# A two-layer H3 (FFT convolution) and MLP kernel: the shift filter goes to TensorE and GpSimd, with a new load order, new homes for the spectra, an inverse transform by halves and finer first blocks

## The chip, the cores and the metric

The kernel runs on one core of one Trainium2 chip. A core has five engines with an instruction queue each: TensorE (PE in the profile; its weight loads are shown apart as PEld), VectorE (DVE), ScalarE (ACT), GpSimd (POOL) and SyncE (SP), which here issues every DMA. The metric is the device time of one execution in microseconds (us). All data are bf16 in on-chip memory; matmul results stand in PSUM as fp32, and only ScalarE and VectorE take them out ("evict").

## The reference

Input is one sequence of 2048 positions and 512 channels. Two layers of an H3 mixer and an MLP follow each other, with the same weights both times:

```python
def _A_ref(q, k, v, shift_k, ssm_k, ssm_D):          # ks = 4, L = 2 * S
    for t in range(ks):                              # causal filter of 4 taps, per channel
        k_shift = k_shift + k_pad[:, t:t + S, :] * shift_k[:, ks - 1 - t][None, None, :]
    kv = k_shift * v
    y = irfft(rfft(kv_pad) * rfft(kf_pad))[:S]       # long causal convolution with ssm_k
    y = y + kv * ssm_D
    return q * y
def _B_ref(x, w1, b1, w2, b2):                       # D = 512, F = 1376
    return gelu(layernorm(x) @ w1 + b1) @ w2 + b2
x = A_q
x = x + _A_ref(layernorm(x), A_k, A_v, ...);  x = x + _B_ref(layernorm(x), ...)
x = x + _A_ref(layernorm(x), A_k, A_v, ...);  x = x + _B_ref(layernorm(x), ...)
```

k, v and the filters are the same in both layers, so y (without q) is computed once and used twice.

## The kernel before, in words

**The front: the convolution.** Channels are taken in four chunks of 128, positions as 16 slices of 128 (position = 16 p + a for partition p, slice a). The long convolution is a transform of length 4096 written as matmuls in two stages forward and two stages back.

1. *The filter's spectrum H.* ssm_k is loaded, ssm_D is added to its first tap on GpSimd (L550), TensorE transposes it (L565), `stage1` multiplies by cosine and sine tables (L580, 16 tiles of 16 matmuls), `stage2` by the table S2 (4 MB, eight loads at L495, matmuls at L593, 16 tiles). Each tile's result is evicted by ScalarE or VectorE (`evac`, L503 and L504). H is then copied by four DMAs with the two halves of its partitions exchanged into HS (real and imaginary part change places).
2. *The shift filter, kv.* Chunks 0 and 1 (`PE_CH`) go through TensorE: k comes transposed by a DMA transpose (L537), GpSimd builds diagonal matrices of the taps (L557), and `shift_pe` adds up four diagonal matmuls a slice in PSUM (L620); VectorE multiplies by v while evicting (L627). Chunks 2 and 3 go through VectorE (`shift_dve`): four multiplications, three additions over 128x2048 and two multiplications by v over 128x1024 a chunk, all at L498, the line of the helper `tt`.
3. *kv's spectrum and the product.* `s1x` runs `stage1` on each chunk into R_GX, `products(hf)` runs `stage2` on two chunks at a time (16 tiles in all, 8 a half), evicts each tile to one of three buffers (R_XB) and multiplies it on VectorE into H and into HS (L498, two products of 128x1024 a tile).
4. *The inverse.* `inverse1(hf)` (L681, 16 tiles of 16 matmuls) writes Z, whose rows hold the columns of both halves side by side, over the place of R_GX; the second inverse stage (L728, eight tiles of four matmuls with 512 columns) writes y.

**The MLP.** Each layer goes through four blocks of four slices. A block does the statistics of x (L746, L748 on VectorE; L752 and L754 on GpSimd for the inverse root), normalises (L760), multiplies by y and adds to x (L498), does the statistics again, normalises into a buffer, transposes it (on TensorE, L798 and an eviction at L806, for the very first block; by a DMA transpose, L790, for all others), then 44 matmuls with W1 (L817), GELU on ScalarE (L822), 44 matmuls with W2 (L835) and the add to x on VectorE (L839). In layer 2 each block's result is written out by one DMA.

**What sets the order.** The program lists its operations with what they read and write; `Prog.schedule` then plays them through with the written durations (`dur`) and gives each engine a fixed order, by earliest start and then by the longest chain behind. DMAs come in program order among those that are ready. Operations that name two engines (`BOTH`) go to the one that ends sooner. PSUM has eight banks; a `Tile` takes two (front) or one (MLP), from a `Pool` with a cap. `sync` and `emit` turn it into five instruction streams with semaphore waits. On the chip each engine, SP too, keeps its order; a late operand holds up everything behind it on that engine. Each GpSimd instruction also waits for the end of the one before it.

**Where things lie.** One array of 105856 bf16 elements a partition is divided by hand, and places are used again: S2's place holds the MLP's activations later; v's place holds x (loaded from q); k's places hold W1 and the inverse table T2; the shift filter's scratch (R_TMP) holds W2; the filter's stage-1 output R_G shares a place with HS, kv's stage-1 output R_GX shares one with Z, kv itself (R_KV) with y (R_YT). A load into a place waits until its last reader is done.

Of the kernel before, what the change touches and what calls it, by code (L numbers as in the profile page):

```python
# [22 lines left out]
class Pool:  # L23


    def __init__(self, nb, cap):
        self.nb, self.cap, self.used = nb, cap, 0
# [17 lines left out]
class Prog:  # L45
# [5 lines left out]
    LAT = 130.0  # L51

    def __init__(self, nc):
        self.nc = nc
        self.ops = []
        self.state = {}
        self.nodes = [(-1, None)]
        self.cache = {}

# [60 lines left out]
    def op(self, eng, fn, dur, reads=(), writes=(), tile=None, dma=None, prio=0.0, nbytes=0, after=()):  # L120
        o = Op()
# [3 lines left out]
        o.extra = prio  # L125
# [47 lines left out]

    def schedule(self):
# [29 lines left out]
        while done < n:  # L204
            best = None
            for e in free:
                te = max(free[e], 0.0)
                cand = None
                for o in ready[e]:
# [3 lines left out]
                    new = [x for x in o.tile if x.base is None]  # L213
                    if new:
# [4 lines left out]
                    k = (s, -o.prio, o.i)  # L219
                    if cand is None or k < cand[0]:  # L220
                        cand = (k, o)
# [4 lines left out]
                if best is None or (cand[0][0], cand[0][0] + d) < best[0]:  # L226
                    best = ((cand[0][0], cand[0][0] + d), e, o, cand[0][0])
# [191 lines left out]
PE_CH = (0, 1)  # L419


def bass_interleave_layers__ssm_conv_h3__mixer_channel_mlp__prompt_kernel(
# [85 lines left out]
    E1 = {ACT: 950.0, DVE: 1200.0}  # L508
# [23 lines left out]
    for i, c in enumerate(PE_CH):  # L532
# [4 lines left out]
        P.op(SP, lambda e, dst=dst, src=src: e.dma_start_transpose(dst, src), 700.0, writes=[dst], dma=True, nbytes=1 << 20)  # L537
# [21 lines left out]
    for b in range(4):  # L559
# [7 lines left out]
        P.op(PE, f, 16 * 62.0, reads=src + [IDN], tile=tl)  # L567
# [3 lines left out]
    def stage1(src, G, gk, g0, dg0, n):  # L571

        for d8 in range(dg0 // 8, (dg0 + n) // 8):
# [8 lines left out]
            P.op(PE, f, 16 * 54.0, reads=[x for y in ins for x in y[2:]], tile=tl)  # L582
# [3 lines left out]
    def stage2(G, ks, n):  # L586
# [8 lines left out]
        P.op(PE, f, len(ks) * 60.0, reads=[x for y in ins for x in y[1:]], tile=tl)  # L595
# [4 lines left out]
    for k8 in range(16):  # L600
        tl = stage2(R_G, range(8 * k8, 8 * k8 + 8), 128)
        evac(BOTH, A(0, 128, R_H + 32 * k8, [4, 8], [512, 32], [1, 4]),
             lambda tl=tl: Q(tl, 0, 128, 0, [128, 8], [4, 32], [1, 4]), E1, tl)
# [26 lines left out]
    def shift_dve(i):  # L630
# [244 lines left out]
```

## Time and profile before

| what | value |
|---|---|
| runs | 275.03, 272.72, 273.45 us; median 273.45 us |
| the profiled execution | 273.39 us |
| its span (first to last instruction) | 271.6 us, 4924 instructions |
| mean granted TensorE clock | 0.953 |
| busy: PE, DVE, ACT, POOL | 233.3, 175.8, 131.7, 30.6 us |
| DMA | 27.35 MB, mean 101 GB/s |
| first MLP matmul, end of the last add | 109.05 us, 268.05 us |

The slices of the page cut the span into 40 parts of 6.8 us; a digit is the busy share of a slice in tenths. A row of the timeline gives start, length, engine, line, operation and operands of a merged run of instructions, and in brackets how long the engine stood idle before it and what ended that. A row of the groups gives a count, the busy time, the mean of one in ns, and the idle time before it. A row of the table of stretches gives the busy time (and count) of PE, PEld, DVE, ACT and POOL in a stretch, then the granted clock, the DMA share and GB/s. "ar" is the on-chip array, "ps" PSUM, "sm" a small array of statistics. Line numbers are those of the kernel before.

### The profile page before, as it was taken

The page shows a single profiled execution, that of the slowest core. Times are in us where ns is not written, and L with a number is a line of the kernel's source. Part 1 is how long each engine was busy: PE and PEld are TensorE (multiplying, and loading weights), DVE is VectorE, ACT ScalarE, POOL GpSimd, SP SyncE. Part 2 cuts the span into 40 slices and gives each one's busy share as a digit, 9 for nine tenths or more (in the row PEclk, how much of TensorE's full clock was granted, in tenths as well). Part 3 has the DMA queues.
Part 4 walks back from the last instruction along what each step waited for, and adds up shares of the span by engine and source line. Part 5 has one row for each costly group of instructions (what it writes and reads, how often), then busy time and mean ns, then how long its engine had stood idle before and what let it go on. Part 6 is the DMA issues. An engine that isn't in the chain of part 4 may idle for free.

```text
span 271.6 us, 4924 instructions
## 1 busy us (share of the span) xinstructions
PE 233.3 (86%) x2080; PEld 131.2 (48%) x2096; DVE 175.8 (65%) x362; ACT 131.7 (48%) x167; POOL 30.6 (11%) x57
## 2 busy tenths in 40 slices
PE   0977997638899731999999999999999999999993
PEld 0966986527899311334344344344333444334441
DVE  0599999678999989989437848749659211101132
ACT  1396099657899842470551542533567030664000
POOL 2460000000101321030101101110110100000000
PEclk9999999977799985699999999999999999999998
DMA  5999985999940000304012022021030401000111
GB/s 171 332 224 386 412 271 123 232 198 275 381 153 2 2 0 1 77 1 77 2 29 48 0 41 39 0 58 23 0 68 9 60 19 77 0 0 31 49 77 77
DMA packets 29923, 27.35 MB, mean 101 GB/s; under 512 B 22384, under 2 KB 26446, under 8 KB 29134
## 3 DMA queue, kind: packets, MB, share of 16 engines
q1 hardware_dynamic: 29902, 27.05, 36.2%
q8 instruction: 16, 0.26, 0.4%
q14 instruction: 5, 0.04, 0.0%
HBM read 16.03 MB, written 2.10 MB: 67 GB/s over the span
## 4 chain that ended last, share of the span: by engine, by line
PE 57%; DVE 24%; DMA 7%; ACT 5%; issue 3%; POOL 2%; SPq 1%; DVEq 0%; ACTq 0%
PE ps L835 26%; PE ps L817 25%; DVE ar L498 11%; DVE sm L746 6%; DMA ar<-ar 5%; ACT ar L503 5%; PE ps L620 3%; DVE ar L504 3%; DVE ar L760 2%; POOL sm L754 2%; PE ps L565 2%; DMA ar<-in_A_ssm_k_dram 2%; PE ps L580 1%; DVE sm L748 1%; DVE ar L839 1%
## 5 line engine op out<-in xcount | busy, mean ns | idle before, releaser
L822 ACT ACTIVATE ar<-ps,sm 128x512 bf16<-128x512 f32 (+1 forms) x88 | 59.5, 687 | 82.5 <-PE ps L817 59.2
L817 PE MATMUL ps<-ar 128*128 128x512 bf16 (+1 forms) x342 | 82.2, 387 | 1.6 <-ACT ar L806 0.8
L503 ACT ACTIVATE ar<-ps 128x1024 bf16<-128x1024 f32 x72 | 67.5, 1045 | 27.4 <-PE ps L593 11.1
L835 PE MATMUL ps<-ar 128*128 128x512 bf16 (+1 forms) x347 | 78.2, 379 | 0.6 <-DVE ar L839 0.3
L498 DVE TENSOR_TENSOR ar<-ar 128x512 bf16<-128x512 bf16 (+2 forms) x114 | 62.4, 606 | 3.8 <-issue 2.9
L839 DVE TENSOR_TENSOR ar<-ar,ps 128x512 bf16<-128x512 bf16 x32 | 21.2, 683 | 65.4 <-PE ps L835 65.4
L817 PEld LDWEIGHTS ps<-ar 128*128 128x128 bf16 (+1 forms) x352 | 31.0, 101 | 50.9 <-ACT ar L822 21.2
L835 PEld LDWEIGHTS ps<-ar 128*128 128x128 bf16 (+1 forms) x352 | 33.7, 98 | 43.2 <-ACT ar L822 2.9
L746 DVE BATCH_NORM_STATS2 sm<-ar 128x6 f32<-128x512 bf16 x64 | 41.5, 683 | 0.1
L760 DVE TENSOR_SCALAR ar<-ar,sm 128x512 bf16<-128x512 bf16 x64 | 23.3, 406 | 11.4 <-POOL sm L754 10.3
L580 PE MATMUL ps<-ar 128*64 128x128 bf16 x512 | 20.1, 231 | 8.8 <-ACT ar L503 7.0
L593 PE MATMUL ps<-ar 128*128 128x64 bf16 (+1 forms) x384 | 19.2, 215 | 4.2 <-issue 1.7
L580 PEld LDWEIGHTS ps<-ar 128*64 128x64 bf16 x512 | 16.4, 116 | 12.2 <-ACT ar L503 9.5
L593 PEld LDWEIGHTS ps<-ar 128*128 128x128 bf16 x384 | 17.6, 107 | 5.8 <-DVE ar L504 2.3
L504 DVE CAST ar<-ps 128x1024 bf16<-128x1024 f32 x16 | 19.0, 1231 | 1.4 <-PE ps L580 1.4
L754 POOL TENSOR_TENSOR sm<-sm 128x4 f32<-128x4 f32 x16 | 16.9, 1059 | 1.3
L752 POOL TENSOR_SCALAR sm<-sm 128x4 f32<-128x4 f32 x16 | 3.3, 207 | 115.7 <-DVE sm L748 115.7
L681 PE MATMUL ps<-ar 128*128 128x128 bf16 x256 | 15.0, 220 | 0.1
L681 PEld LDWEIGHTS ps<-ar 128*128 128x128 bf16 x256 | 14.5, 114 | 0.3 <-ACT ar L503 0.2
L565 PE MATMUL ps<-ar 128*128 128x128 bf16 x64 | 5.9, 270 | 6.5 <-POOL ar L550 6.5
L504 DVE COPY ar<-ps 128x2048 bf16<-128x2048 bf16 x4 | 4.8, 1229 | 9.7 <-PE ps L565 9.7
L798 PE MATMUL ps<-ar 128*128 128x128 bf16 x16 | 2.1, 309 | 9.6 <-DVE ar L760 9.6
(23 smaller groups left out, 62.4 us busy)
## 6 DMA issues: line engine op xcount, KB each, us to landing
ar<-tab_s SPq DMA_DIRECT2D x8, 512.0 KB, 12.7
ar<-ar SPq DMA_DIRECT2D x4, 1024.0 KB, 13.5
ar<-in_A_ssm_k_dram SPq DMA_DIRECT2D x4, 512.0 KB, 5.7
ar<-in_A_v_dram SPq DMA_DIRECT2D x1, 2048.0 KB, 9.3
ar<-in_A_q_dram SPq DMA_DIRECT2D x2, 1024.0 KB, 16.1
out_dram<-ar SPq DMA_DIRECT2D x4, 512.0 KB, 2.6
ar<-in_B_w_dram SPq DMA_DIRECT2D x1, 1376.0 KB, 19.6
ar<-in_B_w_dram SPq DMA_DIRECT2D x1, 1280.0 KB, 17.8
```

What stands on the lines that cost most here:

```text
L498: return P.op(eng, lambda e: e.tensor_tensor(o, a, b, op), dur, reads=[a, b] + list(more), writes=[o])
L503: return e.activation(dst, src(), AF.Copy)
L504: return e.tensor_copy(dst, src())
L580: r = e.matmul(Q(tl, 64 * ri, 64, i * 128, [1, 128]), w, m, start=True, stop=True)
L593: r = e.matmul(Q(tl, 0, 128, i * n, [1, n]), w, m, start=True, stop=True)
L681: r = e.matmul(Q(tl, 0, 128, i * 128, [1, 128]), w, m, start=q == 0, stop=q == 1)
L746: P.op(DVE, lambda e, st=st, x=x: e.bn_stats(st, x), 600.0, reads=[x], writes=[st])
L760: P.op(DVE, lambda e: e.tensor_scalar(o, x, m, r, ALU.subtract, ALU.mult), 260.0, reads=[x, m, r], writes=[o])
L817: r = e.matmul(Q(tl, 0, rows, 0, [1, 512]), w, m, start=dk == 0, stop=dk == 3)
L822: P.op(ACT, lambda e, dst=dst, tl=tl, rows=rows, bias=bias: e.activation(dst, Q(tl, 0, rows, 0, [1, 512]), AF.Gelu_apprx_tanh, bias=bias), ...
L835: r = e.matmul(Q(tl, 0, 128, 0, [1, 512]), ins[fc][0], ins[fc][1], start=fc == 0, stop=fc == 10)
L839: P.op(DVE, lambda e, x=x, tl=tl: e.tensor_tensor(x, x, Q(tl, 0, 128, 0, [1, 512]), ALU.add), 610.0, reads=[x], writes=[x], tile=tl)
```

## The change

- The shift filter: chunks 0, 1 and 2 go through TensorE (`PE_CH = (0, 1, 2)`), chunk 3 through GpSimd (`shift_pool` in place of `shift_dve`: the same seven operations of 128x2048 and two of 128x1024, with two scratch buffers instead of three).
- Load order: one DMA transpose of k stays ahead of v; the other two come behind the eight loads of S2.
- Homes: R_G moves from HS's place to that of R_GX and Z; Z's two halves (by channel) lie apart; a fourth x buffer.
- H's swap is cut in two by columns (kh): eight DMAs of 512 KB in pieces of 512 bytes, four of them as soon as half of H's tiles are evicted.
- The second inverse runs by halves of the channels: per half four tiles of eight matmuls with 256 columns.
- The first layer's blocks are of 2, 2, 4, 4 and 4 slices; the blocks of two use matmuls of 256 columns with W1. Output goes in pieces of two slices.
- The planner: a `Pool` can have a gate (a tile gets its banks only when everything outside the tile that it depends on has been placed), two knobs (`SHY`, `BOOST`) that are zero, and new durations.

```diff
-PE_CH = (0, 1)
+PE_CH = (0, 1, 2)
+BOOST = 0.0
+BLOCKS0, BLOCKS1 = (2, 2, 4, 4, 4), (4, 4, 4, 4)
...
-    R_6, R_7 = place(6144), place(3072)
+    R_6, R_7 = place(6144), place(4096)
...
-    R_G, R_HS = R_2, R_2
+    R_G, R_HS = R_4, R_2
...
-    E1 = {ACT: 950.0, DVE: 1200.0}
+    E1 = {ACT: 940.0, DVE: 1160.0}
...
+    def kt(i):
+
+        c = PE_CH[i]
...
+        P.op(SP, lambda e, dst=dst, src=src: e.dma_start_transpose(dst, src), 5500.0, writes=[dst], dma=True, nbytes=1 << 20)
+
+    kt(0)
     dma(A(0, 128, R_V, [1, 8192]), dr(A_v, 0, [16 * 512, 128], [1, 8192]), 1 << 21)
     for j in range(8):
         tload(t_s2, 128 * 128, j * 2048, R_S2 + j * 2048, 2048)
+    for i in range(1, NPE):
+        kt(i)
     tload(t_sm, row, 384, R_U, 256)
-    dconv = Pool(2, 4)
+    dconv = Pool(2, 4, True)
...
-    for h in range(2):
-        for g in range(2):
-            src, dst = A(64 * g, 64, R_H + 8192 * h, [1, 8192]), A(64 - 64 * g, 64, R_HS + 8192 * h, [1, 8192])
-            dma(dst, src, 1 << 20, reads=[src])
+    for kh in range(2):
+        for k8 in range(8 * kh, 8 * kh + 8):
...
+        for h in range(2):
+            for g in range(2):
+                src, dst = [A(64 * p, 64, r + 8192 * h + 256 * kh, [512, 16], [1, 256])
+                            for p, r in ((g, R_H), (1 - g, R_HS))]
+                dma(dst, src, 3 << 18, reads=[src])
...
-    def shift_dve(i):
+    def shift_pool(i):
...
-               A(0, 128, R_SJ + 512 * i + 128 * j, [0, 16], [1, 128]), ALU.mult, 1200.0,
+               A(0, 128, R_SJ + 512 * i + 128 * j, [0, 16], [1, 128]), ALU.mult, 3500.0, POOL,
                more=halo if j else ())
-        for j in range(3):
-            tap(3 - j, tm[j])
-        tt(tm[1], tm[0], tm[1], ALU.add, 1200.0)
         tap(0, tm[0])
-        tt(tm[2], tm[1], tm[2], ALU.add, 1200.0)
-        tt(tm[1], tm[2], tm[0], ALU.add, 1200.0)
+        for j in range(1, 4):
+            tap(j, tm[1])
+            tt(tm[0], tm[0], tm[1], ALU.add, 3500.0, POOL)
         for q in range(2):
...
-               A(0, 128, R_V + 128 * c + 64 * q, [4, 16], [512, 16], [1, 4]), ALU.mult, 640.0)
+               A(0, 128, R_V + 128 * c + 64 * q, [4, 16], [512, 16], [1, 4]), ALU.mult, 1900.0, POOL)
...
-            evac(BOTH, A(0, 128, R_Z + 32 * d8, [512, 32], [4, 8], [1, 4]),
+            evac(BOTH, A(0, 128, R_Z + 8192 * hf + 32 * (d8 - 8 * hf), [256, 32], [4, 8], [1, 4]),
...
-    for i in range(NPE):
-        shift_pe(i)
-        s1x(PE_CH[i])
-    for i in range(NDV):
-        shift_dve(i)
-        s1x(DV_CH[i])
-    products(0)
-    products(1)
-    inverse1(0)
-    inverse1(1)
+    for c in range(4):
+        P.boost = BOOST if c < 2 else 0.0
+        if c in PE_CH:
+            shift_pe(PE_CH.index(c))
+        else:
+            shift_pool(DV_CH.index(c))
+        s1x(c)
+    for h in range(2):
+        P.boost = BOOST if h == 0 else 0.0
+        products(h)
+        inverse1(h)
...
+    def inverse2(hf):
+        for a4 in range(4):
...
+            for al in range(4):
+                for ri in range(2):
+                    q = (4 * a4 + al) * 2 + ri
+                    ins.append((al, ri, A(0, 128, R_T2 + q * 128, [1, 128]), A(0, 128, R_Z + 8192 * hf + q * 256, [1, 256])))
...
+    P.boost = BOOST
+    inverse2(0)
+    P.boost = 0.0
+    inverse2(1)
...
-        for b in range(4):
-            sl = list(range(4 * b, 4 * b + 4))
+        for n in (BLOCKS0, BLOCKS1)[L]:
+            sl = list(range(s0, s0 + n))
...
-                if L or b:
+                if L or s >= 4:
```

More of the change, by code (lines that the diff above doesn't have):

```diff
@@ L23, with __init__ @@
 class Pool:
-    def __init__(self, nb, cap):
-        self.nb, self.cap, self.used = nb, cap, 0
+    def __init__(self, nb, cap, gate=False):
+        self.nb, self.cap, self.used, self.gate = nb, cap, 0, gate
 class Tile:
@@ L172, in _place, with _gated @@
         return s, got
+    def _gated(self, tile):
+        mine = {x.i for x in tile.ops}
+        return any(p not in mine and self.ops[p].eng is None for x in tile.ops for p in x.preds)
     def schedule(self):
@@ L213, in schedule @@
                     new = [x for x in o.tile if x.base is None]
+                    if any(x.pool.gate and self._gated(x) for x in new):
+                        continue
                     if new:
@@ L594, in f @@
             return r
-        P.op(PE, f, len(ks) * 60.0, reads=[x for y in ins for x in y[1:]], tile=tl)
+        P.op(PE, f, len(ks) * 53.0, reads=[x for y in ins for x in y[1:]], tile=tl)
         return tl
```

100 lines of the change are left out of this document (48 added, 52 removed).

## The prediction, made blind

> **What bounds the kernel now.** I first read the page's slices, then the timeline for the order of the stages.
>
> ```profile
> span 271.6 us, 4924 instructions
> ...
> PE   0977997638899731999999999999999999999993
> DVE  0599999678999989989437848749659211101132
> ACT  1396099657899842470551542533567030664000
> ```
>
> From slice 16 (109 us) on TensorE is full: two layers of MLP. Before that nothing is full throughout: the work goes round between engines. Only the stretch ahead of the first MLP matmul can shrink. The timeline dates its stations (start, length):
>
> ```profile
> 15.55 4.72 DVE L498 TENSOR_TENSOR ar<-ar 128x2048 bf16<-128x2048 bf16 x4
> 24.87 8.20 PE L620 MATMUL ps<-ar 128*128 128x128 bf16 x128 [1.01 <-DVE ar L504]
> 42.94 7.80 SPq L487 DMA_DIRECT2D ar<-ar  x4
> 55.16 4.91 DVE L498 TENSOR_TENSOR ar<-ar 128x1024 bf16<-128x1024 bf16 x8 [2.94 <-issue]
> 64.75 14.54 DVE L498 TENSOR_TENSOR ar<-ar 128x1024 bf16<-128x1024 bf16 x24 [0.80 <-ACT ar L503]
> 73.24 15.01 PE L681 MATMUL ps<-ar 128*128 128x128 bf16 x256
> 89.78 6.85 PE L728 MATMUL ps<-ar 128*128 128x512 bf16 x31 [1.53 <-ACT ar L503]
> 109.05 1.04 PE L817 MATMUL ps<-ar 128*128 128x512 bf16 x2 [0.75 <-ACT ar L806]
> 266.71 1.34 DVE L839 TENSOR_TENSOR ar<-ar,ps 128x512 bf16<-128x512 bf16 x2 [1.69 <-PE ps L835]
> ```
>
> VectorE spends 15 to 50 on the shift filter and on evictions; the filter spectrum is complete at 42.9; its half-swap (four DMAs) follows, and products wait for it until 55; the last product ends at 79.3 (64.75 + 14.54); both inverse stages and one long first block (four slices) follow, and the MLP starts at 109.05, 29.75 us behind the last product. From there to the last add it takes 157.7 us, and 4.9 us more to the end of the span. I leave these almost alone and work out the new start of the MLP, T0.
>
> **Part 1: VectorE loses the shift filter, TensorE gets one chunk.** Rows of the first 115 us by shape (count | busy, mean ns):
>
> ```profile
> L498 DVE TENSOR_TENSOR ar<-ar 128x1024 bf16<-128x1024 bf16 x36 | 22.4, 699 | 3.7 <-issue 2.9 <-ACT ar L503 0.8
> L504 DVE CAST ar<-ps 128x1024 bf16<-128x1024 f32 x16 | 19.0, 1231 | 1.4 <-PE ps L580 1.4
> L498 DVE TENSOR_TENSOR ar<-ar 128x2048 bf16<-128x2048 bf16 x14 | 16.8, 1230 | 0.1
> L627 DVE TENSOR_TENSOR ar<-ps,ar 128x1024 bf16<-128x1024 f32 x4 | 4.8, 1237 | 0.4 <-DMA ar<-in_A_v_dram 0.4
> ...
> L503 ACT ACTIVATE ar<-ps 128x1024 bf16<-128x1024 f32 x72 | 67.5, 1045 | 27.4 <-PE ps L593 11.1 <-PE ps L580 11.0 <-DVE ar L498 3.6
> ```
>
> Gone from VectorE: 14 x 1.230 + 4 x 0.699 = 20.0 us. New on it: two more L627, 2.5 us. TensorE gets 64 more L620 matmuls, 64 x 64 ns (8.20/128) = 4.1 us, in a stretch where it waits for tables. ScalarE loses one small copy. VectorE is thus free to evict: two engines at 1.045 and 1.231 finish a tile each 0.57 us, and the 16 filter tiles of the second stage take 9 us.
>
> **Part 2: load order.** Each DMA transpose occupies SP for 5.5 us, and two of the three now stand behind the V load and the table loads.
>
> ```profile
> ar<-in_A_k_dram SPq DMA_DIRECT2D x1, 1024.0 KB, 9.1
> ...
> 5.32 1.76 SPq L487 DMA_DIRECT2D ar<-in_A_k_dram  x3
> 7.13 11.00 SPq L537 DMA_TRANSPOSE ar<-in_A_k_dram  x2
> 18.17 0.59 SPq L487 DMA_DIRECT2D ar<-in_A_v_dram  x1
> 18.81 4.05 SPq L495 DMA_DIRECT2D ar<-tab_s  x8
> ...
> 27.20:34.00 6.80, 6.80 (x115) 6.80 (x114) 6.42 (x8) 0.45 (x1) 0.00 (x0) 1.00 1.03 413
> 43.50:63.00 19.50, 11.39 (x278) 9.36 (x273) 15.06 (x19) 13.48 (x15) 0.00 (x0) 0.88 1.01 215
> ```
>
> (The last two rows are from the table of stretches; the last number is GB/s.) V is issued at 12.6, the tables from 13.2 to 17.3, 5.5 us earlier. V and tables are 6.3 MB; at 413 GB/s they need 15.2 us behind one transpose that ends near 15: all there at 30 to 31. The filter's second stage keeps pace and ends near 33, against 42.9. The price: transposes two and three hold SP from 17.3 to 28.3 and the DMA queue to about 35, and the swaps stand behind both. The swap moves 4.2 MB, 19.5 us at 215 GB/s: 35 to 54.5, its first half (which no longer waits for the whole spectrum) to 45. It used to run from 43.5 to 63. What hides two other moves: the filter's stage-1 output now lies where kv's goes, so chunk 0's tiles wait for half of the filter's second stage (27), and chunk 1's data are later than that anyway; V is now read last by GpSimd, so q, W1 and W2 (4.8 MB, 12 us) load behind it, from about 55 to 67, and are wanted from 80 on; a GpSimd later by 13 us would uncover them. Chunk 1's data come at 33; its 64 matmuls, one eviction-multiply, and four tiles make the first product possible at about 41, as the first swapped quarter does.
>
> **Part 3: one chunk on GpSimd, the disputed cost.** Seven operations on 128x2048 and two on 128x1024, one after another, each waiting for the one before. No such row exists. The nearest:
>
> ```profile
> 0.72 0.73 POOL L522 MEMSET ar<- 1x768 bf16 x1 [0.29 <-POOLq L860]
> 10.93 7.36 POOL L557 TENSOR_SCALAR ar<-ar,sm 128x128 bf16<-128x128 bf16 x8
> 71.94 0.52 POOL L715 MEMSET ar<- 1x512 bf16 x1 [29.14 <-PE ps L593]
> ...
> L752 POOL TENSOR_SCALAR sm<-sm 128x4 f32<-128x4 f32 x16 | 3.3, 207 | 115.7 <-DVE sm L748 115.7
> ...
> L557 POOL TENSOR_SCALAR ar<-ar,sm x8: 602/603/2476, 10.9 to 15.8; 128x128 bf16<-128x128 bf16 x8
> ```
>
> Below: GpSimd is no faster than VectorE, 1.23 us. Above: the step from 128x4 (207 ns) to 128x128 (603) is 3.19 ns an element, so 2048 cost 6.7 us. Between: a memset grows by 0.81 ns an element (727 less 520 over 256); two operands read in turn at that rate make 3.5 us. I take 3.8, by the stream that it is nearest to, raised towards the other end; 2.0 for the short ones. Sum 7 x 3.8 + 2 x 2.0 = 30.6 us. GpSimd's start: chunk data landed 9.1 us behind issue (15.5); half the bytes, so 14. Of the now 12 diagonal builds (0.603 each) five are done by then; seven, 4.2 us, stand between the taps. End without disturbance: 14 + 4.2 + 30.6 = 48.8.
>
> Disturbance: the eighth L557 took 2476 ns instead of 603; it began at 15.8, inside the row of VectorE products at 15.55. So products with two operands in SBUF and GpSimd exclude each other. Half of the first 16 products (0.7 each) fall inside GpSimd's stretch: 5.6 us. GpSimd ends at 54.4.
>
> The Trainium skill speaks against this change in two places. GPSIMD Engine Reference, section 3.1, gives 4497 ns for an addition over 2048 fp32 elements and advises VectorE for such work; by it the nine operations cost an estimated 36 us and everything below comes 5.5 us later, 259 in all. SBUF — State Buffer, section on the two separate sides, says that the shared ports are locked for a whole instruction and the loser waits it out; the 2476 ns row agrees for GpSimd as the loser, and no row shows VectorE losing.
>
> **Part 4: from GpSimd's end to T0.**
>
> ```profile
> 57.63 0.64 PE L580 MATMUL ps<-ar 128*64 128x128 bf16 x16 [3.70 <-ACT ar L503]
> 62.62 3.70 PE L593 MATMUL ps<-ar 128*128 128x64 bf16 x80
> ```
>
> The last stage-1 tiles: 2 x 0.64 on TensorE and an eviction, 2.3. The first product tile: 0.74 (16 x 46 ns) and an eviction, 1.8. Then 16 products x 0.70 = 11.2. Last product at 54.4 + 15.3 = 69.7 (79.3 before). The swap, done at 54.5, with its four tiles behind it is ready earlier and costs nothing unless it slips by 8 us.
>
> The first inverse is now cut in halves with separate homes: half 0 (7.5 us) and its second inverse (3.5) run while half 1's products do. Behind the last product stand: half 1, 128 x 58.6 ns (15.01/256) = 7.5, and an eviction, 1.3; the first group of the second inverse, eight matmuls of 256 columns, 0.9 at half of 221 ns each, and an eviction, 1.3. That is 80.7. Then a first block of two slices, not four:
>
> ```profile
> L746 DVE BATCH_NORM_STATS2 sm<-ar 128x6 f32<-128x512 bf16 x24 | 15.6, 680 | 0.0
> L498 DVE TENSOR_TENSOR ar<-ar 128x512 bf16<-128x512 bf16 x24 | 9.0, 416 | 0.0
> L760 DVE TENSOR_SCALAR ar<-ar,sm 128x512 bf16<-128x512 bf16 x20 | 7.3, 406 | 2.1 <-POOL sm L754 1.4 <-DMA ar<-ar 0.6
> ...
> L754 POOL TENSOR_TENSOR sm<-sm 128x4 f32<-128x4 f32 x16 | 16.9, 1059 | 1.3
> L748 DVE BATCH_NORM_AGGREGATE sm<-sm 128x2 f32<-128x6 f32 x21 | 3.0, 170 | 0.0
> ...
> 107.26 1.03 PE L798 MATMUL ps<-ar 128*128 128x128 bf16 x8 [5.30 <-DVE ar L760]
> ...
> L806 ACT ACTIVATE ar<-ps 128x512 bf16<-128x512 bf16 x4 | 2.2, 594 | 8.8 <-PE ps L798 8.8
> ```
>
> Per slice two products and one statistic, 1.51; twice 3.0; aggregates 0.3; GpSimd 1.27 and hand-overs 0.2; two norms 0.8; the second slice's transposes 0.5 (1.03/2) and eviction 0.6; remaining hand-overs 0.8: 7.5. T0 = 88.2.
>
> **Part 5: behind T0.** 157.7 stays. Matmuls of 256 columns need half the time of 512 (107 ns), and a weight load with its 128-column matmul takes 58.6, so loads stay hidden. VectorE has done fewer slices in advance (before, eight slices' y lay ahead of T0); a slice costs it two norms, two products, two statistics with aggregates and the last add (0.67), 4.0 us, where TensorE takes 157.7/32 = 4.9, so it follows, with a late third block: 1.5 us, bounds 0 and 5. Output in pieces of two slices: the last is half as big and lands 0.3 sooner. The planner's new durations only change the order; the fourth x buffer, gate and zero-valued knobs I cost at nothing: they issue no instruction. If the order is bad, that is the first rival's price.
>
> **Sum.** 88.2 + 157.7 + 1.5 + 4.9 - 0.3 = 252.0 span. The profiled execution took 273.39 around a span of 271.6, so add 1.8: 253.8 us, against 273.39 and a median of 273.45.
>
> **Rivals.**
> 1. *VectorE loses the port.* Each product waits out a GpSimd operation (3.8 us); since VectorE also evicts, TensorE and ScalarE stand behind it. Four products get through; twelve remain at 50 and end near 58.6, so the first inverse's half 0 moves behind them and collides with half 1's tiles on TensorE (3.5 us). Products end at 71.8, T0 94: 259.5. For: the exclusion row. Against: in that row VectorE was not held up. Chance 0.20.
> 2. *GpSimd at the upper price, slower than before.* 14 + 4.2 + 7 x 6.7 + 2 x 3.5 + 5.6 = 77.7; T0 111.5; 277 us. It decides from 6.2 us an operation on (T0 may slip 19.6 us over an equivalent of eight). For: the only wide GpSimd arithmetic in the trace. Against: a memset streams four times faster. Chance 0.08.
> 3. *The swap in 512-byte pieces.* 512-byte loads ran at 290 GB/s:
>
> ```profile
> 12.00:14.00 2.00, 2.00 (x54) 1.93 (x54) 1.88 (x2) 1.50 (x3) 1.72 (x4) 1.00 1.21 290
> ```
>
> By 290/413 the swap takes 28 us and is ready at 63; with its last four tiles 70.6, almost no harm. At half its rate it is done at 74, products at 82, T0 100.5: 266. Chance 0.08.
> 4. *GpSimd is not the bound.* At 2.5 us or less, swap and TensorE set the last product near 62 to 65; T0 83: 248.5. Chance 0.17.
> 5. *Given back:* T0 comes, but blocks of two starve on VectorE and little is gained, within 1%. For: before T0 VectorE is full in the last slices. Against: 4.0 against 4.9. Chance 0.05.
>
> My forecast has 0.42. **Numbers.** The likeliest is 254. The range 244 to 268 holds the forecast and rivals 1, 3, 4; it leaves out 2 and 5. Slower by over 1% (about what a measurement here tells from none): 0.08; within 1%: 0.05; faster: 0.87.
>
> **What would show it.** GpSimd's tap row near 3.8 us and its last product near 54; VectorE products of a length far over 0.7 during that stretch mean rival 1. The spectrum complete near 33; swaps landed by 55; the first inverse in two runs, one ahead of the last product; first MLP matmul near 88, last add 159 later. It is wrong if T0 comes from something other than GpSimd's end, or if the MLP stretch grows by more than 5 us.

## The result, and the profile after

The changed kernel takes 265.03 us (median of 4 runs, 264.73 to 265.20) against 273.5 for the kernel before: a ratio of 0.968, with a 95% interval of 0.964 to 0.973. It is faster, and the time lies inside the predicted range, but the gain is 8.5 us where 19.5 was forecast. Of experiment 4 below, one execution of four, the profiled one, took 307.87 us at a granted clock of 0.75 against 256.43 to 256.84 us for the others: it is left out, and no trace of that kernel is read.

The profiled execution took 265.0 us. The page's first line and its slices (6.6 us each) stand against those of before; line numbers are now those of the changed kernel, some 11 to 26 higher (L639 is the diagonal matmul that was L620, L646 the eviction that multiplies by v, L574 the diagonal builds, L509 the helper `tt`, L515 VectorE's eviction).

```profile
span 263.2 us, 5244 instructions
...
PE   0999991696669993999999999999999999999995
...
DVE  0597982189899999867998598479479222202223
ACT  1284950058799994656623704605537030583000
POOL 1499999901010231302011101110110100000000
```

GpSimd is full up to slice 7, as was meant. But slice 6 (39 to 46 us) holds three engines that do almost nothing: TensorE 1, VectorE 2, and ScalarE 0 there and in the slice behind. The timeline shows what they wait for (start, length, engine, line, operation; SPq is SP's queue of DMAs):

```profile
18.57 16.83 SPq L550 DMA_TRANSPOSE ar<-in_A_k_dram  x2
36.25 4.18 PE L639 MATMUL ps<-ar 128*128 128x128 bf16 x64 [0.28 <-DMA ar<-in_A_k_dram]
37.38 18.43 SPq L498 DMA_DIRECT2D ar<-ar  x8
...
42.79 0.60 POOL L574 TENSOR_SCALAR ar<-ar,sm 128x128 bf16<-128x128 bf16 x1
43.48 4.04 POOL L509 TENSOR_TENSOR ar<-ar 128x2048 bf16<-128x2048 bf16 x1
47.62 0.60 POOL L574 TENSOR_SCALAR ar<-ar,sm 128x128 bf16<-128x128 bf16 x1
48.31 4.80 POOL L509 TENSOR_TENSOR ar<-ar 128x1024 bf16<-128x1024 bf16 x2
48.33 3.61 PE L639 MATMUL ps<-ar 128*128 128x128 bf16 x32 [7.90 <-issue]
...
52.64 1.94 ACT L514 ACTIVATE ar<-ps 128x1024 bf16<-128x1024 f32 x2 [16.05 <-PE ps L597]
...
58.82 0.68 DVE L509 TENSOR_TENSOR ar<-ar 128x1024 bf16<-128x1024 bf16 x1
```

TensorE ends chunk 1's matmuls at 40.43 and stands 7.90 us, until 48.33: chunk 2's first tile needs a diagonal that GpSimd starts between two of its long operations at 47.62 and ends at 48.22. In TensorE's fixed order, chunk 1's stage-1 tiles (L597) and everything up to the first product stand behind chunk 2's matmuls, so ScalarE idles 16.05 us and the first product starts at 58.82. (The profile puts this wait down to "issue"; the builds' times and the end of the wait, 0.1 us apart, name the cause, and experiment 1 tries it.)

From there VectorE is the limit until the last product, and then the two inverse stages and the first block follow. The first rows below are the timeline, the last is from the table of stretches:

```profile
79.90 4.90 DVE L509 TENSOR_TENSOR ar<-ar 128x1024 bf16<-128x1024 bf16 x8
...
92.04 7.15 PE L749 MATMUL ps<-ar 128*128 128x256 bf16 x64
94.93 1.21 DVE L515 CAST ar<-ps 128x1024 bf16<-128x1024 f32 x1
...
102.80 0.81 PE L828 MATMUL ps<-ar 128*128 128x128 bf16 x8 [3.62 <-DVE ar L787]
104.38 7.76 PE L840 MATMUL ps<-ar 128*128 128x256 bf16 x44 [0.76 <-ACT ar L514]
259.36 1.34 DVE L862 TENSOR_TENSOR ar<-ar,ps 128x512 bf16<-128x512 bf16 x2 [1.69 <-PE ps L858]
```

```profile
57.00:84.80 27.80, 20.76 (x496) 18.43 (x492) 27.10 (x40) 24.00 (x25) 1.90 (x4) 1.00 0.80 243
```

The last product ends at 84.80 (79.29 before). Four stations share the span without a rest:

| stretch | before | predicted | after | after less before |
|---|---|---|---|---|
| start to last product | 79.29 | 69.7 | 84.80 | +5.51 |
| last product to first MLP matmul | 29.76 | 18.5 | 19.58 | -10.18 |
| from there to the start of the last adds | 157.66 | 159.2 | 154.98 | -2.68 |
| from there to the end | 4.89 | 4.6 | 3.84 | -1.05 |
| span | 271.6 | 252.0 | 263.2 | -8.4 |

So the front, which the shift filter's move was to shorten, became longer. The stretch behind the last product, with the finer first block in it, paid for that and for most of the gain.

### The profile page after: what moved, and what is told of

It reads as the page before. It is cut to its first block, busy times and chain, and to the rows that moved or that the text cites. A ratio compares the mean times of both kernels' runs of the same rounds, so it can differ in the third digit from the quotient of the medians.

```text
span 263.2 us, 5244 instructions
## 1 busy us (share of the span) xinstructions
PE 232.6 (88%) x2222; PEld 146.4 (56%) x2236; DVE 169.7 (64%) x355; ACT 126.1 (48%) x168; POOL 65.5 (25%) x75
## 4 chain that ended last, share of the span: by engine, by line
PE 65%; DVE 13%; DMA 7%; SPq 6%; issue 5%; ACT 3%; DVEq 0%
PE ps L840 30%; PE ps L858 28%; DMA ar<-in_A_k_dram 7%; DVE ar L509 6%; PE ps L639 4%; DVE sm L773 4%; ACT ar L514 3%; SPq L550 2%; SPq L498 2%; SPq L506 2%; DVE ar L515 1%; PE ps L610 1%; PE ps L597 1%; DVE ar L787 1%; DVE sm L775 1%
## 5 line engine op out<-in xcount | busy, mean ns | idle before, releaser
L845 ACT ACTIVATE ar<-ps,sm 128x512 bf16<-128x512 f32 (+3 forms) x99 | 61.7, 639 | 75.1 <-PE ps L840 47.4
L514 ACT ACTIVATE ar<-ps 128x1024 bf16<-128x1024 f32 (+1 forms) x67 | 62.5, 1009 | 41.8 <-PE ps L597 27.3
L840 PE MATMUL ps<-ar 128*128 128x512 bf16 (+3 forms) x391 | 80.1, 365 | 1.0 <-ACT ar L514 0.8
L858 PE MATMUL ps<-ar 128*128 128x512 bf16 (+1 forms) x343 | 76.8, 379 | 0.5
L840 PEld LDWEIGHTS ps<-ar 128*128 128x128 bf16 (+1 forms) x396 | 40.8, 104 | 39.3 <-ACT ar L514 1.0
L858 PEld LDWEIGHTS ps<-ar 128*128 128x128 bf16 (+1 forms) x352 | 34.3, 98 | 40.9
L509 DVE TENSOR_TENSOR ar<-ar 128x512 bf16<-128x512 bf16 (+1 forms) x96 | 43.8, 506 | 0.1
L509 POOL TENSOR_TENSOR ar<-ar 128x2048 bf16<-128x2048 bf16 (+1 forms) x9 | 33.3, 3696 | 0.7
L787 DVE TENSOR_SCALAR ar<-ar,sm 128x512 bf16<-128x512 bf16 x64 | 23.1, 404 | 15.1 <-POOL sm L781 12.1
L515 DVE CAST ar<-ps 128x1024 bf16<-128x1024 f32 x25 | 29.5, 1217 | 0.9 <-PE ps L610 0.7
L639 PE MATMUL ps<-ar 128*128 128x128 bf16 x192 | 14.2, 241 | 8.2 <-issue 7.9
L597 PE MATMUL ps<-ar 128*64 128x128 bf16 x512 | 18.0, 224 | 2.3 <-issue 1.2
L639 PEld LDWEIGHTS ps<-ar 128*128 128x128 bf16 x192 | 13.6, 151 | 8.7 <-issue 8.0
L597 PEld LDWEIGHTS ps<-ar 128*64 128x64 bf16 x512 | 15.3, 112 | 4.8 <-issue 1.7
L781 POOL TENSOR_TENSOR sm<-sm 128x4 f32<-128x4 f32 (+1 forms) x18 | 17.1, 949 | 1.5
L646 DVE TENSOR_TENSOR ar<-ps,ar 128x1024 bf16<-128x1024 f32 x6 | 7.4, 1225 | 15.0 <-PE ps L639 15.0
```

What stands on the lines that cost most here:

```text
L509: return P.op(eng, lambda e: e.tensor_tensor(o, a, b, op), dur, reads=[a, b] + list(more), writes=[o])
L514: return e.activation(dst, src(), AF.Copy)
L515: return e.tensor_copy(dst, src())
L597: r = e.matmul(Q(tl, 64 * ri, 64, i * 128, [1, 128]), w, m, start=True, stop=True)
L639: r = e.matmul(Q(tl, 0, 128, a * 128, [1, 128]), w, m, start=j == 0, stop=j == 3)
L787: P.op(DVE, lambda e: e.tensor_scalar(o, x, m, r, ALU.subtract, ALU.mult), 380.0, reads=[x, m, r], writes=[o])
```

## The experiments

All medians are of 4 runs (3 in experiment 4, 10 for the variant with blocks of four), each beside runs of the kernel before on the same chip (273.35 to 273.8). Differences to the changed kernel are those of medians, to 265.03.

**1. The diagonals first.** Theory: TensorE's 7.9 us stand behind diagonals placed between the taps, and everything behind them moves with it. Rivals: the two late transposes and the swap behind them hold the products, or the end of chunk 3 on GpSimd does. The edit changes GpSimd's order alone, once the planner is done:

```diff
     P.schedule()
+    q = P.order[POOL]
+    at = q.index(diags[0])
+    rest = [x for x in q[at:] if x not in diags]
+    q[at:] = sorted(diags, key=lambda x: x.i) + rest
```

> Edit: the twelve diagonal builds stand ahead of the first tap on GpSimd; all other engines keep their order. Theory A (TensorE, in its fixed order, waits for the last diagonal of chunk 2, built at 47.6 between two 4.1 us taps, with chunk 1's stage-1 tiles behind it): the 7.9 us of idle TensorE at 40.4 disappear, the first product comes near 50 instead of 58.8, the total falls by 4 to 7 us, to 258 to 261. Rival B (the two late transposed loads and the swap behind them set the products): within 1 us of 265. Rival C (GpSimd's own end, chunk 3, sets them): the taps start 3.6 us later, so 266 to 269.

Measured: 257.2 us (256.95 to 257.95), ratio 0.939 [0.935, 0.943]: 7.8 us less, a little more than the theory had, by an edit that removes no instruction. Its timeline, and the stretch of its products:

```profile
10.80 8.27 POOL L575 TENSOR_SCALAR ar<-ar,sm 128x128 bf16<-128x128 bf16 x12
19.16 34.29 POOL L509 TENSOR_TENSOR ar<-ar 128x2048 bf16<-128x2048 bf16 x9
...
35.83 6.23 PE L640 MATMUL ps<-ar 128*128 128x128 bf16 x96
...
44.32 2.20 PE L640 MATMUL ps<-ar 128*128 128x128 bf16 x32
...
48.83 2.41 DVE L509 TENSOR_TENSOR ar<-ar 128x1024 bf16<-128x1024 bf16 x1
...
52.30 5.31 DVE L509 TENSOR_TENSOR ar<-ar 128x1024 bf16<-128x1024 bf16 x7
...
71.82 4.90 DVE L509 TENSOR_TENSOR ar<-ar 128x1024 bf16<-128x1024 bf16 x8
...
96.29 7.80 PE L841 MATMUL ps<-ar 128*128 128x256 bf16 x44 [0.84 <-ACT ar L514]
```

```profile
48.80:76.80 28.00, 20.11 (x455) 18.30 (x451) 27.96 (x39) 22.99 (x25) 11.36 (x6) 0.94 1.13 282
```

GpSimd does the same work and ends at 53.45 (53.11 in the changed kernel). The 96 matmuls run without a stop, the first product starts 10.0 us earlier, the last ends 8.1 earlier (76.72), and the MLP starts 8.1 earlier. The theory is shown, and the rivals can't explain it, since neither the transposes (18.51 to 35.08) nor the swap (issued at 37.07) moved forward by more than 0.4 us, and chunk 3's end did not at all.

**2. and 3. The transposes first, alone and with the diagonals.** The edit puts the three transposes behind each other on SP, ahead of V and the tables:

```diff
     P.schedule()
+    q = P.order[SP]
+    at = q.index(kts[0])
+    rest = [x for x in q[at:] if x not in kts]
+    q[at:] = kts + rest
```

> Edit: all three DMA transposes of k stand ahead of v and the tables on SP, as in the kernel before; everything else as in the changed kernel, the diagonals late. Theory A: TensorE still waits for the diagonal until 48.3, total 264 to 267. Rival B: chunks 1 and 2 are there before 20, the swap starts near 36 and ends near 59 instead of 62, total 259 to 262. Rival C: no change, 265.

> Both edits: diagonals first and transposes first. Theory A with B as the next bound: the swap's last quarter lands near 59 and the products follow it; last product near 74 to 77, total 254 to 258. Theory A alone: as with diagonals first alone (258 to 261). Rival B alone: as with the transposes first alone (259 to 262). Rival C: 266 to 269.

Measured: 263.36 us (262.27 to 263.46) alone, ratio 0.960 [0.956, 0.964]; 261.06 (260.97 to 262.62) with the diagonals first, ratio 0.954 [0.949, 0.960]. Alone it takes 1.7 us off the changed kernel and lies between the theory's range (264 to 267) and the rival's (259 to 262). The trace decides for the theory: the MLP starts at 104.25, in the changed kernel at 104.38, so nothing is gained ahead of it. The gain lies in the first block's 44 matmuls, which take 6.25 us instead of 7.76 at a higher granted clock (0.73 instead of 0.50, see the last section). Timelines of the one and of the other:

```profile
7.12 11.29 SPq L550 DMA_TRANSPOSE ar<-in_A_k_dram  x3
...
48.66 3.49 PE L640 MATMUL ps<-ar 128*128 128x128 bf16 x32 [1.94 <-issue]
...
59.02 0.68 DVE L509 TENSOR_TENSOR ar<-ar 128x1024 bf16<-128x1024 bf16 x1
```

```profile
19.15 0.59 SPq L498 DMA_DIRECT2D ar<-in_A_v_dram  x1
...
55.42 0.68 DVE L509 TENSOR_TENSOR ar<-ar 128x1024 bf16<-128x1024 bf16 x1
```

Alone, the same diagonal at 48 us still holds TensorE and the first product stays at 59. With the diagonals out of the way the early transposes cost 3.9 us against experiment 1, where theory A with B had expected a gain (254 to 258): V is issued at 19.15 instead of 13.20, the filter's spectrum is late, and the first product starts at 55.42 instead of 48.83. The changed kernel's load order is right; it only could not show it.

**4. The taps cut short.** Diagonals stay where they are; the seven filter operations on GpSimd take 256 elements a partition in place of 2048, and the two multiplications by v read k unfiltered, so that the filter of chunk 3 is left out.

```diff
-P.op(eng, lambda e: e.tensor_tensor(o, a, b, op), dur, reads=[a, b] + list(more), ...)
+P.op(eng, lambda e: e.tensor_tensor(o2, a2, b2, op), dur, reads=[a, b] + list(more) + ..., ...)
```

> The order of every engine as in the changed kernel; the seven filter operations on GpSimd work on 128x256 instead of 128x2048, and the last two multiply unfiltered k by v (the filter of chunk 3 is left out), so GpSimd is done before 30 instead of 53 and the diagonals come early too. Theory A: as with diagonals first, 258 to 261, because chunk 3 is not what the products wait for. Rival B: within 1 us of 265. Rival C: the products start 15 us earlier or more, 252 or less.

Measured: 256.8 us, ratio 0.937 [0.932, 0.941]. It does to the diagonals what experiment 1 does, by making what stands between them short, and it takes chunk 3's filter nearly away as well. That second thing is worth next to nothing: 256.8 against 257.2. So the end of chunk 3 on GpSimd, on which the forecast's sum hangs, is not what the products wait for.

**5. Blocks of four.** The first layer's blocks as before, all else as changed:

```diff
-BLOCKS0, BLOCKS1 = (2, 2, 4, 4, 4), (4, 4, 4, 4)
+BLOCKS0, BLOCKS1 = (4, 4, 4, 4), (4, 4, 4, 4)
```

> The changed kernel with the first layer's blocks of 4, 4, 4, 4 slices again; nothing else. Theory (the finer first block brings the first MLP matmul nearer to the last product): two more slices of products, statistics and norms on VectorE ahead of it, 3 to 4 us, total 268 to 269. Rival (blocks of two starve and give it back in the MLP): within 1 us of 265.

Measured: 272.85 us (271.90 to 274.18), ratio to before 0.997 [0.995, 1.000]: the rest of the change is worth nothing that can be told. Its timeline:

```profile
80.35 4.90 DVE L509 TENSOR_TENSOR ar<-ar 128x1024 bf16<-128x1024 bf16 x8
...
113.27 11.61 PE L840 MATMUL ps<-ar 128*128 128x512 bf16 x44 [0.75 <-ACT ar L514]
...
266.85 1.34 DVE L862 TENSOR_TENSOR ar<-ar,ps 128x512 bf16<-128x512 bf16 x2 [1.69 <-PE ps L858]
```

The last product stands where the changed kernel has it (85.25), but T0 is 28.0 us behind it instead of 19.6. The blocks of two are worth 7.8 us, about twice what was expected. From T0 to the last adds it takes 153.58 us, 4.1 less than before with the same blocks: the new MLP section gains there by something other than its blocks (its planned durations, which set the order, and its output pieces were not tried apart). The traces show one difference: in the kernel before, TensorE's weight loads for W1 wait 58 times, 21.2 us in all, for GELU on ScalarE; in this variant they don't.

**6. The inverse as before.** Z's rows whole, the second inverse in eight tiles of 512 columns:

```diff
-A(0, 128, R_Z + 8192 * hf + 32 * (d8 - 8 * hf), [256, 32], [4, 8], [1, 4])
+A(0, 128, R_Z + 32 * d8, [512, 32], [4, 8], [1, 4])
-    inverse2(0)
-    inverse2(1)
+    for a2 in range(8):           # the loop of the kernel before
```

> The changed kernel with the inverse as before: Z's rows hold both halves, the second inverse in eight tiles of 512 columns; nothing else. Theory (half 0 of the first inverse runs while half 1's products do): it now waits for all of kv's second stage, the last product to the first MLP matmul grows from 19.6 us by 4 to 7 us, total 269 to 272. Rival (TensorE ran most of half 0 behind the products anyway): within 1.5 us of 265.

Measured: 262.92 us (261.99 to 263.92), ratio 0.960 [0.956, 0.965]: 2.1 us faster than the changed kernel, where it was expected to be slower by some 4 to 7. The kernel with the cut in halves is the slower one. In the changed kernel the first inverse of half 0 does run ahead of the last product, but the second inverse of half 0 doesn't run early: its matmuls stand with half 1's in one run of 64 from 92.04 on. A reading of the traces that no run tried by itself: a tile of half a row holds four slices by 256 channels, so a block of two slices needs two tiles, and one of them is evicted by VectorE (94.93, 1.21 us), which has the first block's statistics to do. With whole rows one tile holds just the first block's two slices and ScalarE evicts it:

```profile
93.02 7.08 PE L748 MATMUL ps<-ar 128*128 128x512 bf16 x32 [1.42 <-ACT ar L514]
95.15 1.43 DVE L509 TENSOR_TENSOR ar<-ar 128x512 bf16<-128x512 bf16 x4 [0.41 <-ACT ar L514]
...
101.32 0.72 PE L821 MATMUL ps<-ar 128*128 128x128 bf16 x8 [1.22 <-DVE ar L780]
102.89 6.64 PE L833 MATMUL ps<-ar 128*128 128x256 bf16 x44 [0.86 <-ACT ar L514]
```

That reading can explain only a part. The two profiled spans are 2.6 us apart: 0.9 us of this lie ahead of the last product (83.94 against 84.80), where the planner's order is another one, 0.6 between it and the first MLP matmul (18.95 against 19.58), and 1.1 in the first 44 MLP matmuls (6.64 against 7.76 us, at a granted clock of 0.66 against 0.50).

**7. and 8. On top of the diagonals first: chunk 3 on VectorE; products evicted by ScalarE alone.**

```diff
-ALU.mult, 3500.0, POOL,      # seven operations; two at 1900.0
+ALU.mult, 1200.0, DVE,       # two at 640.0
```
```diff
-evac(BOTH, A(0, 128, xo, [1, 1024]), ...
+evac((ACT,), A(0, 128, xo, [1, 1024]), ...
```

> The kernel with the diagonals first (257.2 us), and chunk 3's nine operations on VectorE instead of GpSimd. Theory A with VectorE as the bound of the product stage: 9.8 us more on VectorE, of which up to 8 fit its idle stretches before 46 us; the 2.7 us that products waited for the port are gone; total 255 to 261. Rival C (GpSimd's end sets the products): chunk 3 is there earlier, 250 or less. Rival D (every microsecond of VectorE ahead of the last product counts): 264 to 267.

> The kernel with the diagonals first (257.2 us), and the 16 product tiles evicted by ScalarE alone. Theory (32 products and some five evictions of 1.2 us stand one behind the other on a full VectorE): 5 to 6 us off VectorE, last product near 71 to 73 instead of 76.7, total 251 to 254. Rival B (the swap's last quarter, landed at 62, or ScalarE sets the products): within 1 us of 257.

Measured: 256.71 us (256.25 to 256.84) and 257.65 (256.68 to 258.21), against 257.2. Moving one chunk to GpSimd, the edit in the change's name, is worth nothing against leaving it on VectorE, once the diagonals are early. The trace of experiment 7 shows why it comes out even. The first product starts 2.5 us later than in experiment 1:

```profile
51.35 0.68 DVE L509 TENSOR_TENSOR ar<-ar 128x1024 bf16<-128x1024 bf16 x1
```

But no product is held up beside GpSimd any more (the longest of the 32 takes 0.69 us), the stage takes 25.7 us instead of 27.9, and the last product ends at 77.0 against 76.7. The move of chunk 2 to TensorE was not tried alone.

In experiment 8, taking the product tiles' evictions off VectorE doesn't shorten the products, where 5 to 6 us less on VectorE had been expected; the rival has the number. Its timeline:

```profile
48.46 9.23 DVE L509 TENSOR_TENSOR ar<-ar 128x1024 bf16<-128x1024 bf16 x8 [0.30 <-ACT ar L514]
...
57.62 3.60 DVE L515 CAST ar<-ps 128x1024 bf16<-128x1024 f32 x3
...
62.01 14.54 DVE L509 TENSOR_TENSOR ar<-ar 128x1024 bf16<-128x1024 bf16 x24 [0.80 <-ACT ar L514]
```

VectorE does eight products, three evictions that were left to it (of stage-1 tiles: TensorE waits 4.27 us for the first of them, until 58.89), waits 0.80 us for a tile, and does the other 24 products; the last ends at 76.55, as in experiment 1. Only two of the five evictions of experiment 1's stage are gone, 2.4 us. The wait takes 0.8 of that back, and the products lose more to GpSimd: the first eight take 9.23 us, the first two of them beside it, where eight take 4.90 to 4.91 without it. That is a loss of 4.3 us, against 2.8 in experiment 1 (2.41 and 5.31 for eight).

**9. The diagonals first and the inverse as before,** the two edits that helped.

> Diagonals first (257.2 us alone) and the inverse as before (262.9 alone against 265.0 of the changed kernel). If the two are independent, one repairs TensorE's wait before the products and the other the order of the inverse behind them: 257.2 - 2.1 = 255.1, within 254 to 256. If the whole inverse only helped because the products were late, 257 or more.

Measured: 254.67 us (253.33 to 254.99), ratio 0.931 [0.927, 0.935]. This beats both kernels, and it is about what the forecast said for the change itself, but by chance: the MLP starts at 95.49, not at 88.2, and from there to the last adds it takes 152.2 us, not 159.2. The two gains add up: 7.8 + 2.1 = 9.9, measured 10.4. Its timeline (the profiled execution is the fastest of its four):

```profile
72.65 4.29 DVE L509 TENSOR_TENSOR ar<-ar 128x1024 bf16<-128x1024 bf16 x7
...
93.92 0.72 PE L822 MATMUL ps<-ar 128*128 128x128 bf16 x8 [1.22 <-DVE ar L781]
95.49 4.98 PE L834 MATMUL ps<-ar 128*128 128x256 bf16 x44 [0.85 <-ACT ar L514]
```

Against experiment 1's profiled execution, the last product to the first MLP matmul is 1.0 us shorter (18.55 against 19.58), and the first 44 matmuls are 2.8 us shorter (4.98 against 7.80, at a granted clock of 1.00 against 0.50).

**10. The kernel before with the new MLP section only:** blocks of 2, 2, 4, 4 and 4, output in pieces, that section's planned durations; nothing of the front.

```diff
+BLOCKS0, BLOCKS1 = (2, 2, 4, 4, 4), (4, 4, 4, 4)
-        for b in range(4):
-            sl = list(range(4 * b, 4 * b + 4))
+        for n in (BLOCKS0, BLOCKS1)[L]:
+            sl = list(range(s0, s0 + n))
```

> The kernel before with the MLP section of the changed kernel (first layer's blocks of 2, 2, 4, 4, 4, output in pieces of two slices, that section's planned durations); shift filter, loads, homes and inverse as before. Theory E (the finer first blocks carry the whole gain of the change, the rest nets to nothing): 264 to 267. Rival F (the blocks only pay when the inverse runs by halves or VectorE is relieved of the shift filter): 269 to 274.

Measured: 259.25 us (257.81 to 260.24), ratio 0.948 [0.944, 0.953]: 14.1 us off by this alone, more than either theory had, and 5.8 faster than the whole change. Timeline:

```profile
99.62 4.98 PE L814 MATMUL ps<-ar 128*128 128x256 bf16 x44 [0.85 <-ACT ar L504]
...
252.17 1.34 DVE L836 TENSOR_TENSOR ar<-ar,ps 128x512 bf16<-128x512 bf16 x2 [1.69 <-PE ps L832]
```

T0 comes 9.4 us earlier than before, and from there to the last adds it takes 152.55 us instead of 157.66. (The profiled execution, 257.81 us, is the fastest of the four.)

**11. and 12. The swap whole,** as before (four DMAs of rows of 16 KB, after all of the filter's spectrum): on top of experiment 9, and on top of experiment 1.

```diff
-        for h in range(2):
-            for g in range(2):
-                src, dst = [A(64 * p, 64, r + 8192 * h + 256 * kh, [512, 16], [1, 256]) ...
+    for h in range(2):
+        for g in range(2):
+            src, dst = A(64 * g, 64, R_H + 8192 * h, [1, 8192]), A(64 - 64 * g, 64, R_HS + 8192 * h, [1, 8192])
```

> Diagonals first, the inverse as before, and the swap in four DMAs of 16 KB rows at the end of the filter's spectrum instead of eight of 512-byte pieces. If the swap's landing (62 in 512-byte pieces, near 57 to 58 in rows) still holds the products: 251 to 254. If VectorE alone does: as without it, 254 to 256.

> Diagonals first (257.2 us), and the swap in four DMAs of 16 KB rows. Theory (the halves buy nothing, since the swap waits on its queue behind the last transposed load until 37 anyway, and the 512-byte pieces cost 4 us of transfer): the swap lands near 57 to 58; the total 254 to 257. Rival (the first quarter at 45 lets products start early and that counts): 258 to 261.

Measured: 259.60 us (257.70 to 260.79) against 254.67, and 260.85 (260.06 to 261.37) against 257.2. In experiment 11 both ranges are missed, in experiment 12 the rival had it right. The swap in quarters is worth 3.7 to 4.9 us, though it moves its bytes more slowly. The stretches of the two swaps, in the changed kernel and in the last variant, and that variant's first product:

```profile
39.50:61.50 22.00, 12.26 (x241) 11.17 (x240) 9.98 (x11) 5.01 (x5) 13.17 (x6) 0.84 1.15 188
```

```profile
39.50:57.50 18.00, 12.24 (x270) 11.42 (x270) 12.84 (x14) 6.35 (x7) 13.24 (x5) 0.87 1.00 211
```

```profile
51.99 1.61 DVE L509 TENSOR_TENSOR ar<-ar 128x1024 bf16<-128x1024 bf16 x1 [2.73 <-ACT ar L514]
```

It runs at 188 GB/s in pieces and at 211 whole, but the first product then starts at 51.99 instead of 48.83, and the last ends at 81.22 instead of 76.72. (Whole, the swap landed near 62, not near 57 to 58 as expected; in quarters the last one lands near 65 in experiment 1.)

**The sum of the parts,** as steps in this order. Before 273.35 (beside these runs); the new MLP section 259.25 (-14.1); loads, homes, swap, fourth x buffer, the planner's gate and the shift filter, with the diagonals early and the inverse whole, 254.67 (-4.6); the inverse by halves 257.2 (+2.5); the diagonals late 265.0 (+7.8).

## Why the prediction was too low, step by step

**Direction and range: right. The gain: less than half.** The span was forecast at 252.0 and is 263.2, 11.2 longer. By the table of the four stretches above: the last product +15.1, the way to T0 +1.1, the MLP -4.2, the end -0.8.

**Part 1 (VectorE loses the filter): right, and worth nothing for the chunk that was tried.** The operations are gone from VectorE, but experiment 7 puts one of the two chunks back at no cost.

**Part 2 (load order): the size is off.** Transposes two and three held SP for 16.83 us, not 11.0: the first of them, behind V and the tables, 14.07, the other 2.71. (With V and the tables behind them, in experiment 2, they held it for 2.90 and 1.94; the forecast's 5.5 each was a mean of 8.08 and 2.87 in the kernel before.) The swap was issued at 37.4, not at 35, and its last piece landed near 64, not at 54.5. Experiment 3 shows that the order is better by 3.9 us all the same, once the diagonals are early. "Chunk 1's data come at 33": they came at 36.

**Part 3 (GpSimd): the price was right, its place was wrong. This is the step that failed.** The groups by shape of the changed kernel:

```profile
L509 POOL TENSOR_TENSOR ar<-ar 128x2048 bf16<-128x2048 bf16 x7 | 28.5, 4077 | 0.6
...
L574 POOL TENSOR_SCALAR ar<-ar,sm 128x128 bf16<-128x128 bf16 x12 | 7.3, 606 | 1.2
L509 POOL TENSOR_TENSOR ar<-ar 128x1024 bf16<-128x1024 bf16 x2 | 4.7, 2362 | 0.2
```

A tap takes 4.08 us where 3.8 was taken, and GpSimd ends at 53.1 where 54.4 was forecast (that is partly luck, since 5.6 us of the forecast were waits for VectorE's products, and no product ran before that end). GPSIMD Engine Reference, section 3.1, in the Trainium skill, has 4497 ns for such an addition in fp32; in bf16 this trace has 4077, nearer to that page than to the estimate from the memset. The error stands in one clause: of the 12 builds, "seven, 4.2 us, stand between the taps". They were counted as 4.2 us of GpSimd's time. But each is an operand of TensorE. Six were built ahead of the long operations, the planner put the other six one by one between them, and so the last was ready only at 48.2, behind all seven. What stands behind TensorE's wait was not asked: chunk 1's stage-1 tiles, ScalarE, and all products. Experiment 1 measures it: 7.8 us of time, 8.1 of the 15.1 us by which the last product came too late.

**Part 4 (from GpSimd's end to T0): the frame was wrong, the tail right.** The sum lets half of the products run before GpSimd ends and puts "16 x 0.70 = 11.2" behind it. Even in experiment 1, only one of the 32 is done and a second under way when GpSimd ends at 53.45, and the last ends 23.3 us behind that, not 15.3; the four evictions of about 1.2 us that VectorE does among them were not in the sum. Experiments 4 and 7 show that GpSimd's end doesn't set the products. Their start does: from the first to the last product VectorE is full (27.10 of 27.80 us; 27.96 of 28.00 in experiment 1), and that stretch took 26.0 us in the changed kernel and 27.9 in experiment 1, close to the 28.7 that lie between the forecast's 41 and 69.7, which the forecast reached by another sum, so by chance. So the lateness of the first product, 58.8 instead of 41, is all of the +15.1 and more (17.8, less 2.7 for the shorter stretch). With the diagonals early it is 48.8; of the 7.8 us left, 2.8 are the later transpose, and 4.3 are chunk 2's 64 matmuls (a third of the row of 6.23, and 2.20), which TensorE has ahead of the first product's tile in its order.

The tail of 18.5 was right in size (19.6) though one of its premises fell: half 0's second inverse ran no earlier, and with whole rows the kernel is 2.1 to 2.5 us faster (experiments 6 and 9), 0.6 to 1.0 of it in this stretch.

**Part 5 (behind T0): too dear.** 1.5 us more was forecast; it is 2.7 less. Experiment 5 shows the gain with blocks of four, too; that "157.7 stays" for everything but the blocks was not so, and the planned durations and output pieces, put at next to nothing, are what is left to explain it.

**The rivals.** 1 (VectorE loses the port): the effect is there, below, but in the changed kernel no product met a tap, since products start at 58.8 and GpSimd ends at 53.1. 2 and 3: not so; the tap is 4.08 us, the pieces cost 11% of the swap's rate (188 against 211), and the swap landed 21 us ahead of the last product's end. 4 (GpSimd not the bound): its condition, a tap of 2.5 us or less, isn't met; that GpSimd isn't the bound is true all the same, and its time of 248.5 is wrong for the same reason as the forecast, since it let the products start early. 5: not so; the blocks of two don't starve (behind T0 TensorE is busy 154.8 of 155.5 us), and they are what the change gains by.

**What stays open.** Which part of the new MLP section makes it 4.1 us shorter with the old blocks; what the cut in halves does to the clock of the first block; and what chunk 2's move to TensorE, the homes and the planner's gate are worth alone.

## What to carry to other kernels

When small instructions that feed one engine are queued among long ones on another, cost each by when its consumer needs it, not by its own length: 0.6 us of diagonals in the gaps of a stream of 4 us taps cost 7.8 us, and moving them ahead cost nothing. Before moving work off a busy engine, find which event starts the stage that fills it; here, with the swap in quarters, the stage took 25 to 28 us whatever was taken off VectorE; what was taken off bought nothing, and an earlier start did. And try each part of a large change alone: here the new MLP section with its two-slice first block, taken by itself, gives 14.1 us, more than the whole.

## What the runs showed of the hardware

- **VectorE loses the port too.** In experiment 1 the first product starts at 48.83, beside the first of GpSimd's two multiplications by v, and takes 2.41 us, against 0.68 in the changed kernel where GpSimd is idle. It ends at 51.24, 0.55 us after that multiplication. The next seven take 5.31 where seven took 4.29 at the end of experiment 9's stage; again it is one product, beside the second multiplication, that is long (1.70). Before only GpSimd was seen to lose (2476 ns for 603). SBUF — State Buffer in the Trainium skill says, in the section on the two separate sides, that the shared ports are locked for a whole instruction and the loser waits; both directions now agree.
- **The granted clock after a pause.** In the first 5 us of the MLP the clock differs between kernels. The tables of stretches of the changed kernel and of experiment 9:

```profile
104.40:109.40 5.00, 5.00 (x24) 3.57 (x25) 5.00 (x16) 2.37 (x5) 1.03 (x2) 0.50 0.01 3
```

```profile
95.50:100.50 5.00, 4.97 (x44) 4.45 (x46) 5.00 (x15) 4.36 (x10) 1.30 (x2) 1.00 0.00 0
```

  At 0.50 the 44 matmuls of the first block take 7.76 us, at 1.00 they take 4.98. This is the whole difference between the variants behind T0: in experiments 1 to 3, 6 to 9, 11 and 12 and in the changed kernel (experiment 4 aside), the time from the end of these matmuls to the last adds is the same 147.2 us. TensorE had idled 3.62 us shortly before in the changed kernel and 1.22 in experiment 9. Experiments 1, 2, 3, 7, 8 and 12, with 3.6 to 3.8 us of idle time, have 0.50 to 0.73; experiment 10, with 1.5, has 1.00; but experiments 6 and 11 have 0.66 after 1.22. So a long pause was always followed by a low clock here and a short one not always by a full one; what decides is not settled.
- **A DMA transpose's hold on SP depends on the queue.** Behind V and the tables, in the changed kernel, the first of two holds it for 14.07 us and the second for 2.71. Ahead of V, behind the loads of the filters and of k, the first holds it for 6.35 us in experiment 2 and 8.08 in the kernel before, and those right behind it for 1.94 to 2.90.
